# Moving six weight-chunk conversions out of the attention steps of a talking-heads + feed-forward kernel

## The chip, the cores and the metric

The kernel runs on one core of one Trainium2 chip. The metric is the device time of one execution in microseconds (us). The profile comes from one more execution, recorded by the hardware profiler.

## The reference

Two layers run one after the other. The first is "talking heads" attention over 4 batches, 12 heads, 448 positions and head size 64. The second is a feed-forward pair of products over the 1792 rows that attention gives:

```python
scores = scale * np.matmul(q, k.transpose(0, 1, 3, 2))
scores = np.einsum('bhij,hg->bgij', scores, w_pre)     # heads mixed
attn = softmax(scores)                                 # over the last axis
attn = np.einsum('bhij,hg->bgij', attn, w_post)        # mixed again
x = np.matmul(attn, v)                                 # -> 1792 x 768
h = x @ w_in                                           # 768 x 2048
g = where(h >= 1, h, where(h <= -1, 0, (h + 1)**2 / 4))
out = g @ w_out                                        # 2048 x 768
```

w_in and w_out arrive as doubles (8 bytes); everything else is float32.

## The kernel before

**Attention.** The 448 rows of a batch are cut into 4 tiles (120, 120, 120 and 88 rows), and each of the 16 tiles into 3 groups, which gives 48 *steps*. Step n does this, in this order on each engine: SyncE (SP) issues the transfers; TensorE (PE) mixes the heads of group n (`pre`, L221), takes the exponentials of group n-1 into the second mixing (`post`, L261), multiplies a finished tile by v (`pv`, L285), transposes q and k, and computes scores of a later tile (`scores`, L184); VectorE (DVE) takes the row maxima (L225) and evicts; ScalarE (ACT) does the exponentials (L233) and evicts; GpSimd (POOL) adds a small number to the row sums (L240) and scales w_post by their reciprocals (`norm`, L243). The score rows of group n+1 are gathered from one SBUF place (`ssb`) to another (`srows`) by four transfers, `load_s` (L210), issued at the beginning of step n. The places of `srows` are 10, two and a half groups.

**Conversion of the weights.** [...] Each weight matrix is 16 chunks of 128 x 768, and each chunk is turned into float32 and written back to DRAM (`wsd` for w_in, `wod` for w_out). Chunk number 2f is part f of w_in, 2f+1 part f of w_out. One chunk takes, over three steps:

- step n, `conv_load` (L321): three DMAs of 256 KB each, issued by SP just behind `load_s`;
- step n+1: `conv_scaled` (ACT, L329), `conv_bits` (two DVE instructions, L342 and L343), `conv_low` (ACT, L334), `conv_rest` (an addition on POOL, L337);
- step n+2, `conv_store` (L348): one DMA of 384 KB, issued by SP.

The list `CS` (L302) says which steps load a chunk: before, steps 2 to 40 without 3, 6, 15, 18, 27, 30 and 39, so 32 steps for 32 chunks in their order.

**Queues.** All transfers of this part stand in SP's one queue. SP executes it in order: a DMA whose place is not yet free holds all behind it, and issuing a DMA itself takes SP time. The order of the work is written out by hand (`tc.manual_schedule()`); every engine executes its instructions in the order of the program.

**Feed-forward.** The first product is a Strassen-like scheme of 56 *products* j = 0 to 55 (`step(j)`, L514): four quarters of seven with 512 columns each, then four quarters of seven with 384 columns. With k = j mod 7, products 0, 2, 4, 6 of a quarter add into one accumulator bank, 3 and 5 into another. Product j+2 can't write its bank before `evict_f(j)` has read it: ACT does this for k = 0, 2, 3 (L574) and DVE for k = 1, 4, 5 (L576). Within the emission of product j stand, in order: the split of the weights for product j+2 into a high part (ACT, L403) and a low part (DVE, L406), the gates (ACT L542 to L550, DVE L553 to L559), sums of weights and rows (DVE L439, L469), splits of x, and last the eviction. POOL does nothing here. The second product (`mults`, L679) follows, 1176 matmul groups over w_out; it reads parts 10 to 15 of w_out only after it has begun.

Of the kernel before, what the change touches and what calls it, by code (L numbers as in the profile page):

```python
# [11 lines left out]
I32 = mybir.dt.int32  # L12
U32 = mybir.dt.uint32
I64 = mybir.dt.int64
# [8 lines left out]
def tile_talking_heads_moe(  # L23
# [23 lines left out]
    NF = DFF // 128  # L47
    CW = 384
# [12 lines left out]
    qp = s_qk.enter_context(tc.tile_pool(name="qk", bufs=2, side="right"))  # L61
# [14 lines left out]
    for b in range(B):  # L76
        for i0 in range(0, S, QT):
            t = len(tiles)
            n = min(QT, S - i0)
# [6 lines left out]
            if n > 4 * IH * np_:  # L86
                i = (n - 4 * IH * np_) // 2
# [4 lines left out]
    NG = len(groups)  # L92
# [206 lines left out]
        kept[t % 2] = nc.sync.dma_start(out=xd[:, :, b * S + i0:b * S + i0 + n], in_=xo.pop(t)[:, :, :n])  # L299


    CS = [n for n in range(2, NG - 7) if n % 12 not in (3, 6)]  # L302
    craw = {}
    cwt = {}
    cwk = {}

    def conv_ends(i):
        f = i // 2
        if i % 2:
            return w_out[f * 128:(f + 1) * 128, :], wod[f]  # L310
        return w_in[:, f * 128:(f + 1) * 128].rearrange("(k p) f -> p k f", p=128), wsd[f].rearrange("c p d -> p c d")

    def conv_load(i):
        craw[i] = qp.tile([128, 2 * CW], I64, tag="wraw", name="wraw", bufs=2)
        src = conv_ends(i)[0]
        x = craw[i].rearrange("p (k f) -> p k f", f=256 if i % 2 else 128)
        if i % 2:
            src = src.rearrange("p (k f) -> p k f", f=256)
        w = x.shape[1] // 3
        for k in range(0, 3 * w, w):  # L320
            nc.sync.dma_start(out=x[:, k:k + w], in_=src[:, k:k + w])  # L321

    def halves(i):
        w = craw[i].bitcast(I32).rearrange("p (n t) -> p n t", t=2)
        return w[:, :, 0], w[:, :, 1]

    def conv_scaled(i):
        cwt[i] = qp.tile([128, 2 * CW], I32, tag="wt", name="wt", bufs=3)
        nc.scalar.activation(out=cwt[i].bitcast(F32), in_=halves(i)[1].bitcast(F32), func=AF.Copy,  # L329
                             scale=2.0 ** -111)  # L330

    def conv_low(i):
        cwk[i] = qp.tile([128, 2 * CW], I32, tag="wk", name="wk", bufs=1)
        nc.scalar.activation(out=cwk[i], in_=halves(i)[0].bitcast(U32), func=AF.Copy, scale=2.0 ** -29)  # L334

    def conv_rest(i):
        nc.gpsimd.tensor_tensor(out=cwt[i], in0=cwt[i], in1=cwk.pop(i), op=ALU.add)  # L337

    def conv_bits(i):
        hi = halves(i)[1]  # L340
        t = cwt[i]
        nc.vector.tensor_single_scalar(out=t, in_=t, scalar=3, op=ALU.logical_shift_left)  # L342
        nc.vector.scalar_tensor_tensor(out=t, in0=hi, scalar=-0x80000000, in1=t,  # L343
                                       op0=ALU.bitwise_and, op1=ALU.bitwise_or)

    def conv_store(i):
        x = cwt.pop(i).bitcast(F32)
        nc.sync.dma_start(out=conv_ends(i)[1], in_=x if i % 2 else x.rearrange("p (c d) -> p c d", c=2))  # L348

    def conv(n, f):  # L350
        if n in CS and CS.index(n) < 2 * NF:
            f(CS.index(n))


    NA = 1024
# [7 lines left out]
    raw = {}  # L363
# [7 lines left out]
    def view(name, p, off, *dims, dt=F32):  # L371
        n = 1
        for d in dims:
            n *= d
        named[name] = named.get(name, -1) + 1
        x = nc.alloc_sbuf_tensor_at(f"{name}_p{named[name]}", [128, n], dt, offset=area[p] + off).ap()
        if len(dims) == 2:
            x = x.rearrange("p (a b) -> p a b", b=dims[1])
        return x
# [51 lines left out]
    def split_w(j):  # L431
        if j < NJ:
            wts[j] = split_to(raw[KIND[j % 7], j // 7] if j < NJA else raw.pop(j))
# [86 lines left out]
    def step(j):  # L520
        q, k = divmod(j, 7)
        ph = j // NJA
        if k in (0, 1, 3):
            bk[BANK[k]] = bank(3 * (q % 2) if k == 0 else k // 2 + 1)[:, :, :NH[ph]]
        w = wts.pop(j)
        for s in range(2):
            product(bk[BANK[k]][:, s, :], w, s, [xop[ph, k, r] for r in range(3)], k in (0, 1, 3))

    def slot(q, i, h):
        ph = q // NQ  # L530
        return gq[ph, q % NQ].rearrange("p (n i) t -> p n i t", i=2)[:, :, i, h * NH[ph]:(h + 1) * NH[ph]]
# [24 lines left out]
    def take_maxima():  # L556
        while maxima:
            d, x, a = maxima.popleft()
            nc.vector.tensor_tensor(out=d, in0=x, in1=a, op=ALU.max)  # L559
# [5 lines left out]
    def evict_f(j):  # L565
        q, k = divmod(j, 7)
        o = bk[BANK[k]]
        if k == 6:
            bk[q] = o
            return  # L570
        d = slot(q, *((0, 0), (0, 0), (0, 1), (1, 1), (1, 1), (0, 1))[k])
        if k in (0, 2, 3):
            for s in range(2):
                nc.scalar.activation(out=d[:, s], in_=o[:, s, :], func=AF.Copy)  # L574
        else:
            nc.vector.tensor_tensor(out=d, in0=o, in1=d, op=ALU.add)  # L576


    UNITS = ((0, 256), (256, 256), (1024, 256), (1280, 128))
    VOFF = (512, 512, 384, 384)  # L580
# [144 lines left out]
    with tc.manual_schedule():  # L725
# [23 lines left out]
        for m in range(2):  # L749
            x = masks[:, m]  # L750
# [99 lines left out]
        def sx(name, r, k):  # L850
            return lambda: split_xa(name, r, k)
# [24 lines left out]
        for n in range(NG + 2):  # L876
            if n == NE:
# [5 lines left out]
                    name="ps_h", bufs=1, space=PSUM, side="right", reuse_waits="tile"))  # L883
# [15 lines left out]
            j = 0  # L899
# [64 lines left out]
        for j in range(NJ):  # L964
            q, k = divmod(j, 7)
            ph = j // NJA
            end = q == NQ - 1
            if j:
                step(j)
                split_w(j + 2)  # L970
                take_maxima()
            else:
                evict_f(0)
            if k == 0 and q:
                gate_slot(q - 1, 1, 0)
            elif k == 1 and q:
                if ph == 0:
                    sum_w("A21", "A22", "A11", ALU.subtract, q)
                gate_slot(q - 1, 0, 1)
            elif k == 3:  # L980
                gate_slot(q, 0, 0, q not in (0, NQ - 1, NQ))
            elif k == 4 and q:
                gate_slot(q - 1, 1, 1, True)
            if j == 0:
                sum_w("S1", "A21", "A22", ALU.add, 0)
                sx("B12", 2, 4)()
                sx("B11", 2, 3)()
                x_last(2)
                for r, s in enumerate(("s4", "s2", "s6")):
                    load_xa("B22", r, s)  # L990
            elif j == 1:
                sum_w("A21", "A22", "A11", ALU.subtract, q)
            elif j == 2:
                for r in range(3):
                    split_xa("B22", r, 5)
            elif j == 3:
                for r in range(3):
                    split_xa("B21", r, 6)
            if ph == 0:
                if k == 0:  # L1000
                    keep_w(2, q)
                    keep_w(3, q)
                elif k == 2:
                    sum_w("A12", "A12", "A11", ALU.subtract, q)
                    keep_w(4, q)
                    load_b(NJA) if end else load_a("A11", q + 1)
                elif k == 3:
                    keep_w(5, q)
                    load_b(NJA + 1) if end else load_a("A21", q + 1)
                elif k == 4:  # L1010
                    if end:
                        load_b(NJA + 2)
                        load_b(NJA + 3)
                    else:
                        load_a("A22", q + 1)
                        load_a("A12", q + 1)
                elif k == 5 and not end:
                    sum_w("S1", "A21", "A22", ALU.add, q + 1)
                elif k == 6 and not end:
                    sum_w("A11", "S1", "A11", ALU.subtract, q + 1)  # L1020
            load_b(j + 6) if j + 2 >= NJA else None
            if 4 <= j < 7:
                tx_load(j - 4)
            if 6 <= j < 18:
                tx_sum(j - 6)
            if 7 <= j < 19:
                tx_keep(j - 7)
            if 19 <= j < 22:
                for p in range(4):
                    load_xb(4 * (j - 19) + p)  # L1030
            for x in XAT.get(j, ()):
                split_xb(x)
            if j:
                evict_f(j)
            f = j - NJ + 3
            if f == 0:
                load_t(0)
                load_t(1)
            elif f == 1:
                split_t(0)  # L1040
                load_t(2)
                prep_s(0)
            elif f == 2:
                split_t(1)
                load_t(3)
                prep_s(1)
# [62 lines left out]
```

## Time and profile before

| what | us |
|---|---|
| three runs | 862.22, 852.49, 862.94 (median 862.22) |
| profiled execution, its device time | 856.64 |
| its span, first to last instruction | 854.9 |
| attention and the change to the next part, about | 0 to 463 |
| feed-forward, first product, from its last wait but one | 463.5 to 647.3 |
| feed-forward, second product | 647.3 to 854 |
| PE busy | 803.0 (94%) |
| DVE busy | 626.2 (73%) |
| ACT busy | 500.8 (59%) |
| POOL busy | 116.4 (14%) |

PE is the engine that is busy longest. Its busy time is pipelined time: a matmul that waits inside the pipeline counts as busy. The part of the span in which PE could be quicker lies in attention, where its busy share is lower than later.

### The profile page before, as it was taken

The numbers are of one execution on the slowest core, as the hardware profiler recorded it, in microseconds if no ns is written. First come the engines' busy times: TensorE is split into PE (matmuls) and PEld (weight loads), VectorE is DVE, ScalarE is ACT, GpSimd is POOL, SyncE is SP. The second block draws the span as 40 slices with busy tenths as digits, with TensorE's granted clock in tenths as the row PEclk, the third lists the DMA queues.
The fourth block names the chain that finished last, engine by engine and source line by source line (L and its number), as shares of the span: only waits on it lengthen the run. The fifth ranks groups of instructions, "written<-read, shape, count | busy, mean of one in ns | idle before, by whom it ended". The sixth has DMA issues, their size and how long they took to land.

```text
span 854.9 us, 26184 instructions
## 1 busy us (share of the span) xinstructions
PE 803.0 (94%) x11274; PEld 667.4 (78%) x11274; DVE 626.2 (73%) x751; ACT 500.8 (59%) x895; POOL 116.4 (14%) x147
## 2 busy tenths in 40 slices
PE   8799998989989989889789999999999999999998
PEld 6467765667656667557677888899999999999998
DVE  4777876667776767766498797996659978677763
ACT  4576765667666667757545646786666444433431
POOL 4022232222332213322130000000000000000000
PEclk9999999999999999999899999999999999999999
DMA  7688788889889997885826647644433633123331
GB/s 151 201 252 225 235 239 271 255 237 247 249 263 277 238 240 242 269 276 189 242 82 219 243 145 239 207 136 127 127 126 130 222 129 125 54 91 111 124 117 65
DMA packets 139091, 162.87 MB, mean 191 GB/s; under 512 B 42252, under 2 KB 128480, under 8 KB 138976
## 3 DMA queue, kind: packets, MB, share of 16 engines
q1 hardware_dynamic: 138464, 160.50, 61.8%
q8 instruction: 89, 1.46, 0.7%
q0 software_dynamic: 256, 0.47, 0.3%
q10 hardware_dynamic: 256, 0.23, 0.1%
q14 instruction: 26, 0.21, 0.1%
HBM read 88.81 MB, written 33.82 MB: 143 GB/s over the span
## 4 chain that ended last, share of the span: by engine, by line
PE 71%; DMA 11%; ACT 5%; DVE 5%; SPq 4%; issue 3%; POOLq 1%; POOL 0%; ACTq 0%; DVEq 0%
PE ps_f L679 24%; PE ps_f L514 21%; DMA srows<-ssb 8%; PE ps_a L261 7%; PE ps_l L221 6%; PE ps_x L285 5%; PE ps_s L184 4%; ACT e L233 2%; SPq L210 2%; PE ps_k L148 2%; DVE nm L225 1%; DMA kraw<-in_k_dram 1%; SPq L321 1%; DVE ssb L190 1%; PE ps_t L169 1%
## 5 line engine op out<-in xcount | busy, mean ns | idle before, releaser
L233 ACT ACTIVATE e<-ps_l,nm 128x448 f32<-128x448 f32 x180 | 112.0, 632 | 52.4 <-DVE nm L225 52.0
L261 PEld LDWEIGHTS ps_a<-wr,e 60*64 60x64 f32 (+1 forms) x5760 | 103.5, 129 | 48.2 <-issue 26.9
L225 DVE TENSOR_REDUCE nm<-ps_l 128x2 f32<-128x896 f32 (+1 forms) x92 | 95.3, 1063 | 41.9 <-PE ps_l L221 38.1
L261 PE MATMUL ps_a<-wr,e 60*64 60x60 f32 (+2 forms) x5760 | 111.9, 219 | 14.8 <-ACT e L233 7.4
L221 PE MATMUL ps_l<-srows,wpre 64*64 64x448 f32 (+2 forms) x720 | 101.8, 561 | 16.4 <-DMA srows<-ssb 7.6
L662 ACT ACTIVATE sgh_p<-gq_p 128x1024 fp32r<-128x1024 f32 (+1 forms) x56 | 53.3, 953 | 89.8 <-PE ps_f L679 89.6
L406 DVE SCALAR_TENSOR_TENSOR wl<-wi,wh 128x768 fp32r<-128x768 f32 x71 | 67.7, 953 | 41.9 <-ACT wh L403 41.9
L679 PE MATMUL ps_f<-wh,sgl_p 128*128 128x384 f32 x294 | 98.2, 334 | 0.0
L679 PE MATMUL ps_f<-wh,sgh_p 128*128 128x384 f32 x294 | 98.2, 334 | 0.0
L679 PE MATMUL ps_f<-wl,sgh_p 128*128 128x384 f32 x294 | 98.2, 334 | 0.0
L403 ACT ACTIVATE wh<-wi 128x768 fp32r<-128x768 f32 x71 | 59.7, 842 | 57.8 <-DVE wi L626 18.0
L663 DVE TENSOR_TENSOR sgl_p<-gq_p,sgh_p 128x1024 fp32r<-128x1024 f32 (+1 forms) x56 | 60.9, 1088 | 35.0 <-ACT sgh_p L662 35.0
L221 PEld LDWEIGHTS ps_l<-srows,wpre 64*64 64x64 f32 (+2 forms) x720 | 26.6, 134 | 70.2 <-issue 18.5
L285 PE MATMUL ps_x<-aT,v 112*64 112x120 f32 (+1 forms) x1408 | 77.3, 262 | 2.4 <-issue 2.4
L192 ACT ACTIVATE aT<-ps_a 112x960 f32<-112x960 f32 (+1 forms) x44 | 41.8, 950 | 53.0 <-PE ps_a L261 52.7
L285 PEld LDWEIGHTS ps_x<-aT,v 112*64 112x64 f32 x1408 | 67.9, 137 | 5.7 <-issue 3.1
L190 DVE COPY ssb<-ps_s 120x896 f32<-120x896 f32 (+1 forms) x48 | 52.0, 1084 | 22.8 <-PE ps_s L184 14.0
L337 POOL TENSOR_TENSOR wt<-wt,wk 128x768 int32<-128x768 int32 x32 | 58.1, 1816 | 53.3 <-ACT wk L334 51.4
L190 DVE COPY aT<-ps_a 112x960 f32<-112x960 f32 x48 | 55.0, 1145 | 3.0 <-PE ps_a L261 3.0
L679 PEld LDWEIGHTS ps_f<-wh,sgh_p 128*128 128x128 f32 x294 | 55.2, 188 | 0.0
L679 PEld LDWEIGHTS ps_f<-wl,sgh_p 128*128 128x128 f32 x294 | 55.2, 188 | 0.0
L679 PEld LDWEIGHTS ps_f<-wh,sgl_p 128*128 128x128 f32 x294 | 55.2, 188 | 0.0
(211 smaller groups left out, 1653.1 us busy)
## 6 DMA issues: line engine op xcount, KB each, us to landing
srows<-ssb SPq DMA_DIRECT2D x176, 210.0 KB
wraw<-in_moe_w_in_dram SPq DMA_DIRECT2D x48, 256.0 KB
wraw<-in_moe_w_out_dram SPq DMA_DIRECT2D x48, 256.0 KB
wi<-wod SPq DMA_DIRECT2D x29, 384.0 KB
wi<-wsd SPq DMA_DIRECT2D x28, 384.0 KB
wsd<-wt SPq DMA_DIRECT2D x16, 384.0 KB
wod<-wt SPq DMA_DIRECT2D x16, 384.0 KB
wi<-wss SPq DMA_DIRECT2D x16, 384.0 KB
```

The source lines that it names most:

```text
L190: nc.vector.tensor_copy(out=out, in_=in_)
L221: nc.tensor.matmul(out=ps[h, j, :S], lhsT=wpre[p], rhs=x[p], start=True, stop=True)
L225: nc.vector.tensor_reduce(out=nm, in_=lps[m][:, :k, :S], axis=AX.X, op=ALU.max, negate=True)
L233: nc.scalar.activation(out=e, in_=ps[:, j, :S], func=AF.Exp, bias=nm[:, j:j + 1], accum_out=sm[:, j:j + 1])
L261: nc.tensor.matmul(out=o[h, r, :, :n, j], lhsT=e[p, r * KP + h.start:r * KP + h.stop], rhs=w[p].rearrange("p (g i) -> p g i", i=IH)[:, :, :n],
L285: nc.tensor.matmul(out=ps[half[s], m, :n], lhsT=vt[b, g][:, 2 * m + s, r * D:(r + 1) * D], rhs=a[:KP, r * H + h, :n], start=(r == 0), stop ...
L337: nc.gpsimd.tensor_tensor(out=cwt[i], in0=cwt[i], in1=cwk.pop(i), op=ALU.add)
L403: nc.scalar.activation(out=hi, in_=t, func=AF.Copy, scale=2.0 ** -8)
L406: nc.vector.scalar_tensor_tensor(out=lo, in0=t, scalar=2.0 ** -8, in1=hi.bitcast(F32), op0=ALU.mult, op1=ALU.subtract)
L514: nc.tensor.matmul(out=o, lhsT=u[:, c, k], rhs=x, start=first and r == 0 and m == 0, stop=r == 2 and m == 2, skip_group_check=True)
L663: nc.vector.tensor_tensor(out=lo, in0=src, in1=hi.bitcast(F32), op=ALU.subtract)
L679: nc.tensor.matmul(out=o, lhsT=x[:, f, c], rhs=y[:, f % 2, :], start=first and f == 0 and m == 0, stop=hf == 1 and f == 3 and m == 2, skip ...
```

## The change

Ten of w_out's chunks stay in attention, placed between w_in's 16 by a list `CONV`; the last six, parts 10 to 15, are converted during the first feed-forward product by `late_conv(j)`, called in the emission of product j behind `evict_f(j)`. Steps divisible by three no longer load a chunk: against before, steps 9, 12, 21, 24, 33 and 36 lose theirs, and the 26 others stay. The late chunks use fixed SBUF places that no other tile holds at that time; the intermediate of `conv_low` is written in place, over the low halves of the doubles.

```diff
-    CS = [n for n in range(2, NG - 7) if n % 12 not in (3, 6)]
+    LATE = 6
+    CONV = [2 * f for f in range(NF)]
+    for f in range(NF - LATE):
+        CONV.insert(2 * f + 2 + f // 2, 2 * f + 1)
+    CS = [n for n in range(2, NG - 7) if n % 3]
...
-        if n in CS and CS.index(n) < 2 * NF:
-            f(CS.index(n))
+        if n in CS:
+            f(CONV[CS.index(n)])
...
+    RAWS = (("gg", 32768), ("gg", 49152), ("gg", 58368), ("xc", 12288), ("xc", 18432))
+    LOWS = (("gg", 38912), ("gg", 55296), ("gg", 55296), ("xc", 9216), ("xc", 9216))
+    LCONV = ((7, 10, 0), (9, 13, 1), (12, 17, 2), (27, 30, 3), (30, 34, 4), (34, 38, 3))
+
+    def late_conv(j):
+        for m, (j0, j1, x) in enumerate(LCONV):
+            i = 2 * (NF - LATE + m) + 1
+            if j == j0:
+                conv_load(i, view("cr", *RAWS[x], 2 * CW, dt=I64))
+            elif j == j1:
+                conv_scaled(i, view("ct", *LOWS[x], 2 * CW, dt=I32))
+                conv_bits(i)
+            elif j == j1 + 1:
+                conv_low(i, halves(i)[0])
+                conv_rest(i)
+            elif j == j1 + 2:
+                conv_store(i)
...
             if j:
                 evict_f(j)
+            late_conv(j)
```

## Rows read from the trace of the kernel before

**Rows 1.** The page: shares of the span of the chain that ended last.

```profile
PE 71%; DMA 11%; ACT 5%; DVE 5%; SPq 4%; issue 3%; POOLq 1%; POOL 0%; ACTq 0%; DVEq 0%
```

**Rows 2.** Windows between the L240 of steps 3, 12, 16, 24, 28; 36, 40, 42.

```profile
core 0: us, PE busy (x) PEld busy (x) DVE busy (x) ACT busy (x) POOL busy (x), PEclk, DMA share, GB/s
49.69:122.58 72.89, 70.35 (x1753) 52.00 (x1753) 56.28 (x72) 53.45 (x109) 20.85 (x25) 1.00 0.82 239
122.58:161.94 39.36, 33.03 (x699) 21.90 (x697) 27.05 (x34) 24.47 (x54) 11.11 (x13) 0.96 0.81 254
161.94:232.70 70.76, 66.77 (x1571) 47.77 (x1570) 50.81 (x64) 47.91 (x98) 18.05 (x23) 1.00 0.90 249
232.70:270.18 37.48, 32.28 (x700) 21.01 (x698) 26.85 (x34) 24.16 (x54) 11.16 (x13) 1.00 0.84 264
...
342.43:379.96 37.53, 32.20 (x699) 21.54 (x699) 26.87 (x35) 24.34 (x54) 11.03 (x13) 0.95 0.85 268
379.96:394.79 14.83, 14.53 (x382) 10.61 (x382) 11.13 (x14) 10.85 (x24) 3.60 (x5) 1.00 0.63 207
```

**Rows 3.** Timeline of SP: start us, us, what it issues and how many.

```profile
115.12 4.40 SPq L321 DMA_DIRECT2D wraw<-in_moe_w_out_dram  x3
...
120.10 0.45 SPq L348 DMA_DIRECT2D wod<-wt  x1
120.65 4.54 SPq L210 DMA_DIRECT2D srows<-ssb  x4
125.29 2.75 SPq L321 DMA_DIRECT2D wraw<-in_moe_w_in_dram  x3
```

**Rows 4.** The chain that ended last, pieces in order: start us, us, what.

```profile
21.22 4.90 DMA srows<-ssb
...
124.42 5.30 DMA srows<-ssb
```

**Rows 5.** Tiles wraw and wt, SP's issues: count, ns minimum/median/maximum, first and last start.

```profile
L321 SPq DMA_DIRECT2D wraw<-in_moe_w_out_dram x48: 356/846/2063, 50.8 to 377.4; - x48
...
L348 SPq DMA_DIRECT2D wod<-wt x16: 326/448/1607, 73.0 to 394.0; - x16
```

**Rows 6.** The page, DMA issues: count, KB each.

```profile
wraw<-in_moe_w_out_dram SPq DMA_DIRECT2D x48, 256.0 KB
...
wod<-wt SPq DMA_DIRECT2D x16, 384.0 KB
```

**Rows 7.** Tile wt: the conversion's instructions, columns as in Rows 5.

```profile
L329 ACT ACTIVATE wt<-wraw x32: 884/906/942, 49.5 to 387.2; 128x768 f32<-128x768 f32 x32
L342 DVE TENSOR_SCALAR wt<-wt x32: 525/528/560, 50.7 to 389.2; 128x768 int32<-128x768 int32 x32
L343 DVE SCALAR_TENSOR_TENSOR wt<-wraw,wt x32: 1022/1224/1360, 51.3 to 389.8; 128x768 int32<-128x768 int32 x32
L337 POOL TENSOR_TENSOR wt<-wt,wk x32: 1799/1817/1837, 53.6 to 392.2; 128x768 int32<-128x768 int32 x32
```

**Rows 8.** Windows as in Rows 2: products 14 to 20, and products 28 to 34.

```profile
500.85:529.67 28.82, 28.82 (x127) 23.62 (x126) 23.20 (x27) 17.29 (x21) 0.00 (x0) 1.00 0.56 194
...
558.49:580.33 21.84, 21.84 (x128) 21.84 (x127) 20.40 (x28) 16.59 (x25) 0.00 (x0) 1.00 0.41 125
```

**Rows 9.** Timeline of DVE about products 39 to 41: start us, us, what, idle before.

```profile
595.70 0.96 DVE L406 SCALAR_TENSOR_TENSOR wl<-wi,wh 128x768 fp32r<-128x768 f32 x1 [3.21 <-ACT wh L403]
...
597.45 0.95 DVE L576 TENSOR_TENSOR gq_p<-ps_f,gq_p 128x768 f32<-128x768 f32 x1
```

**Rows 10.** Timeline of PE: the first matmul of product 41.

```profile
599.05 0.34 PE L514 MATMUL ps_f<-b6h_p,wl 128*128 128x384 f32 x1
```

**Rows 11.** Timeline of POOL: two of the instructions that scale w_post.

```profile
117.08 0.55 POOL L243 TENSOR_TENSOR wr<-wpost,rs 128x120 f32<-128x120 f32 x1 [1.42 <-DVE rs L241]
...
125.51 0.74 POOL L243 TENSOR_TENSOR wr<-wpost,rs 128x240 f32<-128x240 f32 x1 [2.70 <-DVE rs L241]
```

**Rows 12.** Timeline of DVE at the same two places.

```profile
117.42 1.02 DVE L343 SCALAR_TENSOR_TENSOR wt<-wraw,wt 128x768 int32<-128x768 int32 x1
...
125.84 1.22 DVE L343 SCALAR_TENSOR_TENSOR wt<-wraw,wt 128x768 int32<-128x768 int32 x1
```

More of the change, by code (lines that the diff above doesn't have):

```diff
@@ L311, in conv_ends, with conv_load @@
         return w_in[:, f * 128:(f + 1) * 128].rearrange("(k p) f -> p k f", p=128), wsd[f].rearrange("c p d -> p c d")
-    def conv_load(i):
-        craw[i] = qp.tile([128, 2 * CW], I64, tag="wraw", name="wraw", bufs=2)
+    def conv_load(i, raw=None):
+        craw[i] = qp.tile([128, 2 * CW], I64, tag="wraw", name="wraw", bufs=2) if raw is None else raw
         src = conv_ends(i)[0]
@@ L325, in halves, with conv_scaled, conv_low @@
         return w[:, :, 0], w[:, :, 1]
-    def conv_scaled(i):
-        cwt[i] = qp.tile([128, 2 * CW], I32, tag="wt", name="wt", bufs=3)
+    def conv_scaled(i, t=None):
+        cwt[i] = qp.tile([128, 2 * CW], I32, tag="wt", name="wt", bufs=3) if t is None else t
         nc.scalar.activation(out=cwt[i].bitcast(F32), in_=halves(i)[1].bitcast(F32), func=AF.Copy,
                              scale=2.0 ** -111)
-    def conv_low(i):
-        cwk[i] = qp.tile([128, 2 * CW], I32, tag="wk", name="wk", bufs=1)
+    def conv_low(i, k=None):
+        cwk[i] = qp.tile([128, 2 * CW], I32, tag="wk", name="wk", bufs=1) if k is None else k
         nc.scalar.activation(out=cwk[i], in_=halves(i)[0].bitcast(U32), func=AF.Copy, scale=2.0 ** -29)
```

## The prediction

> **What bounds the kernel now.** Start with the page's chain of waits: PE has 71% of it, but DMA 11% and SP's queue 4% [rows 1]. So some of the end is set by transfers and by their issue, and the question is where. The windows cut at step boundaries answer it [rows 2]. Steps 40 and 41, where the DMA share is down to 0.63, take 14.83 us, 7.4 us each, and PE fills them. Four such steps would be 29.7 us. But the four steps from 12 take 39.36, those from 24 take 37.48 and those from 36 take 37.53 [rows 2]: 9.7, 7.8 and 7.8 us over PE's own pace, 25.3 us in three places I call the *zones*. Outside them there is less to win: 72.89 us from step 3 to 12 with PE busy 70.35, and 70.76 with 66.77 from 16 to 24 (the stretch from 28 to 36 is like it).
>
> Why the zones are slow shows in SP's timeline [rows 3]: a store, four gathers and three chunk loads follow one another without a pause, 0.45, 4.54 and 2.75 us, and the chunk before took 4.40. A step's transfers alone fill 8 us or more of SP's queue, against PE's 7.4. The gather of srows stands on the chain [rows 4], and it is issued late because chunk transfers stand ahead of it. The DMA engines are busy too: share 0.81 to 0.85, at 254 to 268 GB/s [rows 2]. Either way PE waits for srows, and a chunk is what makes the step too full.
>
> In the first feed-forward product it is the reverse: PE busy 28.82 of 28.82 and 21.84 of 21.84, DMA share 0.56 and 0.41, POOL idle, but DVE busy 23.62 and 20.40 [rows 8]. Here every microsecond of PE stall goes to the end.
>
> **What is removed, part by part.** Steps 12, 24 and 36 lose a chunk inside a zone; 9, 21 and 33 three steps ahead of one. A chunk costs SP three loads and a store: at the medians 3 x 0.846 + 0.448 = 2.99 us [rows 5], at the fullest place 4.40 + 0.45 = 4.85 [rows 3]. For the DMA engines it is 3 x 256 + 384 KB, 1.18 MB [rows 6], which at 264 GB/s [rows 2] take 4.5 us. The ACT, DVE and POOL work of those steps goes as well, but none of them is full there (24.47, 27.05 and 11.11 of 39.36 [rows 2]), so I give it nothing; it lies beside the wait for srows, and if that wait went entirely, PE would be next.
>
> Bounds: at least the zone's own chunk at the lower price, 3 x 2.99 = 9 us; at most all six at 4.5, 27 us, which is also about all that the zones have (25.3). I take for each zone its own chunk at 4.5, because SP and DMA are both full there, and half of 2.99 for the chunk three steps earlier, because SP still has some waits in those steps and its lead is limited by the ten places of srows: 6 us a zone, **18 us** in all, nearer the middle.
>
> The reordering (w_in's chunks sooner, w_out's late) costs nothing: w_in is complete at step 42, as before, and w_out's last parts are read only in the second product, after 647 us; were that cover gone, PE would wait there for a chunk's transfers, about the 4.5 us above.
>
> **What is added.** Six conversions beside the first product. Each brings two ACT passes (0.906 us each), 0.528 + 1.224 us on DVE, 1.817 us on POOL [rows 7], and four DMAs. The transfers I cost at nothing: shares of 0.56 and 0.41 leave room [rows 8], and the loads are issued three or more products ahead of their use. The store makes SP wait for POOL, and behind it stand weight loads for products at least two ahead; POOL needs 1.8 us of a product's 28.82 / 7 = 4.1, so it should be done when SP arrives. If not, one product waits, 3 to 4 us.
>
> ACT and DVE are another matter, since they execute in program order. Take products 38 to 41 [rows 9, 10]. DVE idles 3.21 us until ACT has split the weights for product 41, at 595.70; it then evicts product 39 at 597.45 to 598.40, and product 41 needs that bank at 599.05. The slack is 0.65. The change puts `conv_scaled` ahead of ACT's split (0.9 us later) and `conv_bits` ahead of DVE's low part: 1.75 us, which begin only when ACT has scaled, near 595.7. The eviction then ends some 1.8 us later, and PE stalls for 1.8 - 0.65 = 1.15 us. The places at products 10 and 17 have the same k = 3 and the same order; I give them the same. Three places make 3.5 us; for the three others (13, 30, 34), where no such tight eviction follows at once, 0.5 together. **4 us.**
>
> Then POOL. L343 reads two SBUF tensors. Beside a POOL instruction that ended at 126.25 it ended at 127.06; beside one that ended at 117.63, at 118.44 [rows 11, 12]. Both times it ends 0.81 us after POOL does, and takes 1.22 or 1.02 accordingly: it was held until POOL had finished. In attention the longer addition L337 falls beside DVE instructions that read PSUM. In the first product most of DVE's work reads two SBUF tensors, so L337's 1.82 us can hold it. Two or three of the six additions will fall into a DVE pause like the 3.21 us of [rows 9]; the others, where DVE is busy 23.20 of 28.82 or 20.40 of 21.84 [rows 8], delay it by up to 1.82 each. Three of them: 5.5, of which I take **5 us**.
>
> The Trainium skill's page "SBUF — State Buffer", section "SBUF: two separate sides", speaks against this change: VectorE and GpSimd share one pair of ports as an exclusive lock, and a VectorE instruction with two SBUF inputs and a GpSimd instruction that reads SBUF shut each other out for their whole length. The trace agrees [rows 11, 12]. If every one of the six additions shut DVE out and all of that reached PE, the cost would be 6 x 1.82 = 10.9 instead of 5 and the sum 854; without the lock it would be 843.
>
> Bounds of what is added: 0, if all is hidden (PE can't gain here, it is full), and 6 x (2 x 0.906 + 1.752 + 1.817) = 32 us, if nothing is.
>
> **Sum.** 856.64 - 18 + 4 + 5 = 847.6, say 848 us. That is against the profiled execution, which lies 5.6 us below the median of the three runs and 4.2 above the lowest.
>
> **The rivals.**
>
> *Everything comes off and POOL holds nobody.* Attention gains 26, the product loses only 4: 856.64 - 26 + 4 = 835. For it: the zones have room for 25 us. Against: the chunk of step 9 lies where PE is already busy 70.35 of 72.89 [rows 2], and rows 11 and 12.
>
> *The gather's own latency remains.* A gather took 4.90 us at the very start, when little else was in flight, and 5.30 in the zone [rows 4]; what is left to win by less traffic is 0.4. If issue is not what delays it, each zone gains only half a chunk's issue, 1.5, and the whole 4.5: 856.64 - 4.5 + 9 = 861. Against it: the pauseless SP queue [rows 3].
>
> *Slower: DVE's queue in the first product.* Evictions, low parts and gates all stand behind the late conversions and behind POOL's lock. If the delays don't drain before the next chunk, each costs its whole 5.4 us: 32 us, and 856.64 - 18 + 32 = 871; with attention's gain at its lower bound 880. It decides from 3 us of stall a chunk on (18 / 6). For it: DVE at 20.40 of 21.84 in products 28 to 34, which hold two of the six. Against: DVE has pauses in the other quarters.
>
> *The change doesn't do what it says:* the late chunks' places are not free, SP is held at product 7, and weight loads behind it come late. Attention's work on PE ends before product 1, so this is unlikely; a stall of three products would give 860.
>
> **How the numbers follow.** Forecast 0.52 (its own range 841 to 857, from 9 to 24 us gained and 3 to 12 lost), all comes off 0.20, latency remains 0.17, slower 0.08, held places 0.03. The 2% are about what a measurement of this kernel can tell from no change: 17 us, so below 839.5 or above 873.8 on the profiled execution's basis. Faster by more: the second case and the edge of the first, 0.25. Slower by more: the upper half of the slower case, 0.05. Between: 0.70. The range for 8 in 10 runs from 836 to 864: it takes in the forecast, the latency case and half of the case of 835, and leaves out the other half and the slower case.
>
> **What would show it.** In the changed kernel's windows the zones should shrink from 39.4, 37.5 and 37.5 us to about 33, with pauses in SP's timeline before the steps divisible by three; the stretch from step 3 to 12 should stay near 73. Between products 11 and 42 PE should show stalls of 0.5 to 2 us, released by DVE's evictions or low parts, 9 us together, and L406 or L439 instructions stretched beyond 0.95 us beside L337. I am wrong if the zones stay at 37 or more, if the first product's stalls pass 18 us, or if they are nearly absent.

## The result, and the profile of the changed kernel

| | kernel before | changed kernel |
|---|---|---|
| median of 20 runs, us | 861.88 (852.05 to 866.61) | 852.35 (845.89 to 859.67) |
| ratio, 95% interval | | 0.9909 (0.9883 to 0.9936) |
| profiled execution, us | 856.64 | 857.77 |
| its span, us | 854.9 | 856.1 |

The change takes off 0.9%, 9.5 us between the medians, and the interval leaves out 1. **The two profiled executions don't show it**: before's lies 5.2 us below its median, the changed kernel's 5.4 above. Stages have to be compared, and over several profiles.

The windows are cut as in [rows 2]; behind the six of attention, from step 3 to step 40, stands one from the first matmul of product 7 to that of product 55. Columns as there.

```profile
48.19:129.34 81.15, 73.18 (x1758) 54.76 (x1760) 54.83 (x71) 52.15 (x108) 18.80 (x24) 0.96 0.76 213
129.34:163.57 34.23, 31.55 (x694) 20.56 (x694) 25.20 (x32) 22.55 (x52) 9.13 (x11) 1.00 0.85 255
163.57:235.34 71.77, 66.83 (x1578) 49.51 (x1578) 49.21 (x63) 46.02 (x96) 16.05 (x21) 0.98 0.81 229
235.34:271.32 35.98, 30.66 (x699) 21.19 (x699) 25.01 (x33) 22.45 (x52) 9.15 (x12) 0.95 0.82 247
271.32:335.61 64.29, 62.87 (x1573) 46.84 (x1574) 48.92 (x63) 46.09 (x96) 16.07 (x22) 1.00 0.86 247
335.61:369.69 34.08, 29.86 (x694) 20.90 (x693) 25.18 (x32) 22.61 (x52) 9.15 (x11) 1.00 0.86 250
464.12:645.14 181.02, 173.97 (x866) 156.30 (x864) 148.81 (x168) 124.93 (x176) 11.86 (x6) 0.99 0.60 197
```

The zones went from 39.36, 37.48 and 37.53 [rows 2] to 34.23, 35.98 and 34.08. The first stretch is 8 us longer, at a granted clock of 0.96. The last row is the price: before, products 7 to 55 took

```profile
472.01:643.99 171.98, 171.02 (x865) 155.09 (x864) 134.55 (x156) 116.06 (x164) 0.00 (x0) 1.00 0.51 166
```

so 9.04 us were added there. PE waits (engine, line, what it waited for: us in all, times, longest) from product 7 to 55; before, one of 1.0 us for ACT's L574 stood there:

```profile
PE ps_f L518 <- DVE gq_p L580: 4.4, 4, 2.4
PE ps_f L518 <- ACT gq_p L578: 2.6, 2, 1.6
```

All releasers are evictions, DVE's and ACT's. The page's chain of waits, against [rows 1], says the same by shares: it can be followed back only over 46% of the span, the two products, and DVE, ACT, DMA and issue hold 11% of the span in it. Before, PE alone held as long a part (L514 21%, L679 24%).

```profile
PE 35%; DVE 5%; DMA 2%; issue 2%; ACT 2%; SPq 0%; DVEq 0%; ACTq 0%
```

**The order, at product 41.** DVE's timeline about products 39 to 41, to be laid beside [rows 9], and then PE's:

```profile
595.88 0.56 DVE L346 TENSOR_SCALAR ct_p<-ct_p 128x768 int32<-128x768 int32 x1 [3.14 <-ACT ct_p L333]
596.48 0.96 DVE L347 SCALAR_TENSOR_TENSOR ct_p<-cr_p,ct_p 128x768 int32<-128x768 int32 x1
597.35 0.95 DVE L410 SCALAR_TENSOR_TENSOR wl<-wi,wh 128x768 fp32r<-128x768 f32 x1
...
599.09 0.95 DVE L580 TENSOR_TENSOR gq_p<-ps_f,gq_p 128x768 f32<-128x768 f32 x1
```

```profile
600.10 0.45 PE L518 MATMUL ps_f<-b6h_p,wl 128*128 128x384 f32 x1 [0.74 <-DVE gq_p L580]
```

The conversion's two instructions come out of the pause first; the low part and the eviction follow 1.5 us later than they would, and product 41 waits 0.74 us for the eviction.

**The lock, at three additions.** POOL's timeline, and DVE's at the same places:

```profile
488.89 1.86 POOL L341 TENSOR_TENSOR ct_p<-ct_p,cr_p 128x768 int32<-128x768 int32 x1 [58.22 <-ACT cr_p L338]
...
521.46 1.88 POOL L341 TENSOR_TENSOR ct_p<-ct_p,cr_p 128x768 int32<-128x768 int32 x1 [18.87 <-ACT cr_p L338]
570.07 2.46 POOL L341 TENSOR_TENSOR ct_p<-ct_p,cr_p 128x768 int32<-128x768 int32 x1 [46.73 <-DMA cr_p<-in_moe_w_out_dram]
```

```profile
489.57 2.00 DVE L410 SCALAR_TENSOR_TENSOR wl<-wi,wh 128x768 fp32r<-128x768 f32 x1 [0.43 <-ACT wh L407]
...
522.09 2.06 DVE L410 SCALAR_TENSOR_TENSOR wl<-wi,wh 128x768 fp32r<-128x768 f32 x1 [0.88 <-ACT wh L407]
...
569.83 0.96 DVE L558 TENSOR_TENSOR gq_p<-gq_p,ga_p 128x768 f32<-128x768 f32 x1
570.70 3.18 DVE L466 TENSOR_TENSOR b6l_p<-xr_p,b6h_p 128x384 fp32r<-128x384 f32 x3
```

L410 takes 0.95 us elsewhere; beside POOL's addition it takes 2.00 and 2.06, and ends 0.8 us after POOL. At 570 the holding goes both ways: POOL's addition is itself 0.6 us longer, while L558 finishes, and the three L466 behind it take 3.18 us together instead of 1.49. That is the costliest place: product 34, which needs the bank that DVE evicts next (L580 at 574.68), waits until 575.68, and then runs at a lower clock. Windows of the changed kernel: products 28 to 34, to be laid beside [rows 8], and the wait and what follows it:

```profile
554.41:580.47 26.06, 23.68 (x127) 23.35 (x126) 24.90 (x32) 19.14 (x29) 2.46 (x1) 0.93 0.63 211
...
571.00:575.60 4.60, 2.29 (x14) 1.97 (x12) 4.60 (x6) 4.42 (x5) 1.53 (x1) 1.00 0.15 52
575.60:580.50 4.90, 4.82 (x19) 4.83 (x20) 3.95 (x6) 0.90 (x1) 0.00 (x0) 0.65 0.75 244
```

DVE is busy without a gap for 4.60 of 4.60 us, PE for 2.29; then the granted clock is 0.65 for 4.9 us. The quarter takes 26.06 us instead of 21.84. The lower clock is this profile's alone. In E2 and E12 (below), product 34 waits as long, but the 4.9 us behind the wait ran at 1.00, and the quarter took 24.5 us. E12's window:

```profile
573.80:578.70 4.90, 4.90 (x28) 4.90 (x29) 3.94 (x5) 1.21 (x2) 0.00 (x0) 1.00 0.82 245
```

### The profile page after: what moved, and what is told of

It is laid out like the page before. It is cut to its first block, busy times and chain, and to the rows that moved or that the text cites. A ratio compares the mean times of both kernels' runs of the same rounds, so it can differ in the third digit from the quotient of the medians.

```text
span 856.1 us, 26225 instructions
## 1 busy us (share of the span) xinstructions
PE 800.6 (94%) x11274; PEld 671.0 (78%) x11274; DVE 630.5 (74%) x751; ACT 499.9 (58%) x895; POOL 116.3 (14%) x147
## 5 line engine op out<-in xcount | busy, mean ns | idle before, releaser
L225 DVE TENSOR_REDUCE nm<-ps_l 128x2 f32<-128x896 f32 (+1 forms) x92 | 94.8, 1063 | 37.2 <-PE ps_l L221 35.8
L221 PE MATMUL ps_l<-srows,wpre 64*64 64x448 f32 (+2 forms) x720 | 91.6, 552 | 6.0 <-DMA srows<-ssb 2.5
L410 DVE SCALAR_TENSOR_TENSOR wl<-wi,wh 128x768 fp32r<-128x768 f32 x71 | 71.8, 1014 | 26.3 <-ACT wh L407 26.3
L285 PE MATMUL ps_x<-aT,v 112*64 112x120 f32 (+1 forms) x1408 | 79.8, 265 | 9.3 <-issue 9.3
L285 PEld LDWEIGHTS ps_x<-aT,v 112*64 112x64 f32 x1408 | 69.4, 139 | 12.6 <-issue 9.9
L243 POOL TENSOR_TENSOR wr<-wpost,rs 128x240 f32<-128x240 f32 (+2 forms) x48 | 37.1, 772 | 128.3 <-DVE rs L241 113.2
```

The lines of the kernel that those rows point to most:

```text
L221: nc.tensor.matmul(out=ps[h, j, :S], lhsT=wpre[p], rhs=x[p], start=True, stop=True)
L225: nc.vector.tensor_reduce(out=nm, in_=lps[m][:, :k, :S], axis=AX.X, op=ALU.max, negate=True)
L285: nc.tensor.matmul(out=ps[half[s], m, :n], lhsT=vt[b, g][:, 2 * m + s, r * D:(r + 1) * D], rhs=a[:KP, r * H + h, :n], start=(r == 0), stop ...
L410: nc.vector.scalar_tensor_tensor(out=lo, in0=t, scalar=2.0 ** -8, in1=hi.bitcast(F32), op0=ALU.mult, op1=ALU.subtract)
```

## The experiments

The time of each kernel is given as its ratio to the kernel before, run on the same chip. "Products" is the stretch from product 7 to 55 in its profile: 172.0 us before; with the change 181.0, and 179.4 in E12. The edits of E5, E6, E7 and E11 are shown against the kernel before, the others against the changed kernel; for E10 E1's edit comes with it. E1, E5, E6 and E10 leave chunks out, and their second product reads other parts of w_out in their place.

**E1. Attention's part alone.**

```diff
-            late_conv(j)
...
+        f -= 6 if f >= NF - LATE else 0      # wo() reads other parts
```

> The attention part of the change alone: 26 chunks in attention, none beside the first product; where the second product would read the last six parts of w_out it reads six other parts. Theory (attention gains 18 us, the late conversions cost 9): 862 - 18 = 844 us, the first product as before, 172 us from product 7 to 55. Rival (attention gains no more than the 9.5 us that the whole change measured, and the late conversions cost nothing in the median): 852 us. Second rival, lower bound of attention's gain, 9 us: 853.

0.9788 (0.9733 to 0.9842), 841.79 us: 18 us off. Products 172.0. Its zones took 32.6, 36.8 and 34.8. The window from step 28 to 36, of the kernel before and then of E1:

```profile
270.18:342.43 72.25, 66.49 (x1578) 48.20 (x1576) 50.76 (x65) 47.88 (x98) 18.02 (x22) 1.00 0.89 245
...
260.17:325.58 65.41, 63.50 (x1570) 47.13 (x1571) 48.78 (x62) 46.01 (x96) 16.04 (x21) 1.00 0.85 239
```

The size is the forecast's. The place isn't: this stretch, which was to have little to win, went from 72.25 to 65.41, and PE's busy time in it from 66.49 to 63.50.

**E2. The late conversions alone.** All 32 chunks in attention as before, and the six converted once more late.

```diff
...
-    CS = [n for n in range(2, NG - 7) if n % 3]
+    CONV = list(range(2 * NF))
+    CS = [n for n in range(2, NG - 7) if n % 12 not in (3, 6)]
```

> The late conversions alone: all 32 chunks in attention as before, and the six last parts of w_out converted a second time at the places of the change. Theory: the first product takes 9 us more from product 7 to 55 (172 to 181 us) and the kernel 862 + 9 = 871 us. Rival (late conversions hidden): 862 us. Rival (they cost their whole work, 5.4 us each): 894 us.

1.0096 (1.0060 to 1.0132), 8 us more; products 179.4. E1 and E2 multiply to 0.988, against 0.991 for the change: as far as these intervals tell, the two parts don't touch each other.

**E3. Without POOL's addition in the late chunks.**

```diff
-                conv_rest(i)
+                cwk.pop(i)
```

> The changed kernel with POOL's addition of the six late chunks left out (their lowest bits are missing); everything else stays, the two ACT passes and two DVE instructions too. Theory (POOL's additions hold DVE, 5 of the 9 us): the first product takes 176 us from product 7 to 55 instead of 181, the kernel 852 - 5 = 847 us; the stalls at products 18 to 19 and 33 to 34 shrink most, those at 13, 20 and 41 stay. Rival (only the order on ACT and DVE counts): 181 us and 852 us, no stall gone.

0.9902 (0.9857 to 0.9946), a time that can't be told from the change's. The products can: 175.7, and the waits in them (the same view as for the changed kernel) are

```profile
PE ps_f L518 <- DVE gq_p L580: 2.1, 4, 1.0
PE ps_f L518 <- ACT gq_p L578: 1.7, 3, 1.0
```

So the order costs 3.7 (175.7 - 172.0), and POOL's addition the rest, 3.7 to 5.3 by the three profiles with all of it (179.4, 179.4, 181.0). The 5.3 contains the lower clock behind product 34. By the spacing of the products, the addition reaches PE at two places only: product 19 begins 1.4 us sooner without it, and product 34 2.2 us.

**E4. The same six at other places**, three of them behind the eviction (the flag 1), three ahead of the split of the weights (0); the addition always behind the eviction.

```diff
+    LCONV = ((7, (10, 0), (12, 1), 0), (9, (14, 0), (16, 1), 1), (12, (19, 0), (19, 1), 2),
+             (27, (33, 1), (34, 1), 3), (30, (36, 1), (37, 1), 4), (35, (39, 1), (41, 1), 3))
```

> The changed kernel with the late conversions at other places: ACT and DVE passes ahead of the weights' split at products 10, 14 and 19 and behind the eviction at 33, 36 and 39; the low half with POOL's addition at 12, 16, 19, 34, 37 and 41, where DVE has pauses in the trace. The same work in all. Theory (the 9 us are a matter of where DVE is tight): stalls of 1 to 3 us instead of 9, 173 to 175 us from product 7 to 55, the kernel 852 - 7 = 845 us. Rival (the cost is the work itself on full engines): still 181 us and 852 us.

0.9863 (0.9799 to 0.9927); products 178.4, not clearly better. ACT's timeline after the chunk at product 14, ahead of product 19, which waits 1.7 us:

```profile
499.11 0.85 ACT L407 ACTIVATE wh<-wi 128x768 fp32r<-128x768 f32 x1 [3.73 <-DVE wi L443]
499.86 1.14 ACT L546 ACTIVATE ga_p<-gq_p,cs 128x1024 f32<-128x1024 f32 x1
...
503.19 1.07 ACT L578 ACTIVATE gq_p<-ps_f 128x512 f32<-128x512 f32 x2
```

In this stretch DVE has no pause, and POOL's addition, from 495.46 to 497.33, holds DVE as well:

```profile
495.81 2.34 DVE L410 SCALAR_TENSOR_TENSOR wl<-wi,wh 128x768 fp32r<-128x768 f32 x1
```

So DVE's weight sum L443 comes late, ACT's split waits 3.73 us for it, three gate passes follow, and only then the eviction (L578). A delay on DVE can come back by way of ACT's queue.

**E5 and E6. Which chunks count.** Before, without the chunks of steps 12, 24, 36 (E5) or 9, 21, 33 (E6).

```diff
+    CS = [n for n in range(2, NG - 7) if n % 12 not in (0, 3, 6)]   # E5
+    CS = [n for n in range(2, NG - 7) if n % 12 not in (3, 6, 9)]   # E6
```

> The kernel before with the chunks of steps 12, 24 and 36 left out alone (three parts of w_out are not converted; the second product reads other parts in their place). Theory of the prediction (a zone gains 4.5 us by its own chunk, 1.5 by the one three steps earlier): 13.5 of 18 us, 860 - 13.5 = 846 us. Rival (all six chunks are worth the same, 3 us each): 851 us. Rival (nothing but the sum of the traffic counts, and the gain is spread over the stretch behind): the zones shrink by less than 2 us each.

> The kernel before with the chunks of steps 9, 21 and 33 left out alone. Theory of the prediction: 4.5 of 18 us, 855 us. Rival (all six are worth the same): 851 us, as without 12, 24 and 36.

E5: 0.9963 (0.9927 to 0.9999), 3 us off. E6: 0.9892 (0.9848 to 0.9936), 9 us off. So the chunk three steps ahead is worth 3 us, twice what was forecast. The chunk inside a zone comes out at 1 instead of 4.5, but the two intervals overlap (0.9927 to 0.9936), and E8 below, with the same attention as E5, gives 3. That the second three are worth more than the first isn't shown.

**E7. SP relieved, bytes unchanged.** Before, with the chunk loads issued by POOL.

```diff
-            nc.sync.dma_start(out=x[:, k:k + w], in_=src[:, k:k + w])
+            nc.gpsimd.dma_start(out=x[:, k:k + w], in_=src[:, k:k + w])
```

> The kernel before with the three loads of every chunk issued by POOL instead of SP; the same bytes, the same steps, stores still on SP. If SP's issue time is what makes a step too full (2.54 us of it a chunk), the zones shrink by about 4 us each, PE's waits for srows go and the kernel is 10 us faster or more, 850 us. If the traffic on the DMA engines is what counts, the zones stay at 37 to 39 us and the kernel at 860 us. If POOL's queue adds waits of its own (behind the additions, or for w_post's scaling), it is slower than 860.

1.0222 (1.0189 to 1.0254), 19 us slower. SP's timeline in the first zone now has pauses, between 131.6 and 133.0 and after 133.4:

```profile
126.85 4.73 SPq L210 DMA_DIRECT2D srows<-ssb  x4
133.04 0.32 SPq L133 DMA_DIRECT2D qraw<-in_q_dram  x1
139.57 0.35 SPq L348 DMA_DIRECT2D wod<-wt  x1
```

and the zone takes 40.79 us all the same (39.36 before), with a granted clock of 0.87:

```profile
128.77:169.56 40.79, 34.75 (x706) 24.28 (x706) 26.98 (x34) 24.59 (x54) 16.62 (x22) 0.87 0.80 241
```

**E8 and E9. Fewer late chunks, in DVE's pauses.** E8 leaves steps 12, 24, 36 free and converts three chunks late. E9 leaves all six but step 24, and converts four chunks whole and one in two halves.

```diff
+    CS = [n for n in range(2, NG - 7) if n % 12 not in (0, 3, 6)]   # E8
+    LCONV = ((7, (10, 0), (12, 1), 0), (12, (17, 0), (19, 1), 2), (34, (38, 0), (40, 1), 3))
...
+    CS = [n for n in range(2, NG - 7) if n % 3 or n == 24]   # E9
+    LCONV = ((7, (10, 0), (12, 1), 0), (12, (17, 0), (19, 1), 2), (27, (33, 1), (34, 1), 3), (34, (38, 0), (40, 1), 4),
+             (43, (45, 0), (47, 1), "h0"), (49, (52, 0), (54, 1), "h1"))
```

> Three late chunks instead of six: steps 12, 24 and 36 lose theirs, and parts 13 to 15 of w_out are converted beside the first product ahead of the weights' split at products 10, 17 and 38 (the pauses of 3.2 to 3.6 us of DVE), POOL's additions at 12, 19 and 40. Theory: attention gains 13.5 us, the first product loses 1 to 2 us: 860 - 12 = 848 us, better than the change. Rival (all six worth the same): 860 - 9 + 1.5 = 852 us, no better than the change.

> Five late chunks, all in DVE pauses: whole chunks at products 10, 17, 33 and 38, one in two halves at 45 and 52 (ACT and DVE ahead of the weights' split except at 33, POOL's addition two products later, one at 33); step 24 keeps its chunk, the other steps divisible by three have none. Theory (attention gains 15 of 18 us; in the pauses a late chunk costs 0.4 us, as with three late ones, and 0.8 at 33): 860 - 15 + 3 = 848 us, 174 to 175 us from product 7 to 55, 4 us better than the change. Rival (late work costs what it costs wherever it stands, 1.5 us a chunk): 180 us in the first product, 852 us.

E8: 0.9908 (0.9874 to 0.9943), 8 us off, products 173.2. Up to product 7 its instructions are those of E5. E8 does 1.2 us more in the products and is still 4 to 5 us faster than E5, so its attention gained 9 us where E5's gained 3; why is open. With E8, the chunks inside the zones (9 us) and those ahead (E6, 9 us) add up to E1's 18, 3 us each. E9: **0.9842 (0.9795 to 0.9890), 846.83 us, the fastest of the kernels that do the whole work**; products 173.98 for five chunks. In time its interval overlaps that of the change, run beside it (E12); the products, 5.4 us fewer, are the clear part. DVE's timeline of E9 at products 10 to 12:

```profile
474.14 0.56 DVE L346 TENSOR_SCALAR ct_p<-ct_p 128x768 int32<-128x768 int32 x1
474.73 0.96 DVE L347 SCALAR_TENSOR_TENSOR ct_p<-cr_p,ct_p 128x768 int32<-128x768 int32 x1
...
479.76 0.96 DVE L410 SCALAR_TENSOR_TENSOR wl<-wi,wh 128x768 fp32r<-128x768 f32 x1 [2.73 <-ACT wh L407]
...
482.24 1.22 DVE L580 TENSOR_TENSOR gq_p<-ps_f,gq_p 128x1024 f32<-128x1024 f32 x1
...
484.68 2.95 DVE L563 TENSOR_TENSOR gq_p<-gq_p,ga_p 128x1024 f32<-128x1024 f32 x1
```

The bits now stand before the pause, and the pause is still 2.73 us long. The addition falls behind the eviction L580; it still holds DVE (L563 takes 2.95 instead of 1.21), but nobody waits for that.

**E10. The order of the chunks.** E1 with its chunks in the order of their numbers.

```diff
+    CONV = [i for i in range(2 * NF) if not (i % 2 and i > 2 * (NF - LATE))]
```

> As the run with the attention part alone, but the 26 chunks in the order of their numbers (w_in and w_out in turn), not w_in ahead. The removals of three steps each gave 3.2 and 9.3 us, 12.5 in sum, all six with the new order 18.2. Theory (order costs nothing, the gains of six don't add up from threes): 842 us. Rival (the order is worth the rest): 860 - 12.5 = 847 us.

0.9789 (0.9736 to 0.9841): the same as E1, within the 5 us of the interval either way. No cost and no gain of the reordering shows.

**E11. One load of 768 KB a chunk instead of three**, else before.

```diff
-        for k in range(0, 3 * w, w):
-            nc.sync.dma_start(out=x[:, k:k + w], in_=src[:, k:k + w])
+        nc.sync.dma_start(out=x, in_=src)
```

> The kernel before with one load of 768 KB a chunk instead of three of 256 KB; the same bytes. If SP's issue time makes the steps too full, SP is relieved by up to 1.7 us a chunk, the zones shrink by 2 us each and the kernel is 5 us or more faster, 855 us. If the DMA engines' traffic counts, the zones stay and the kernel stays at 860 us, or becomes slower where gathers come to stand behind one long transfer.

1.0106 (1.0057 to 1.0156), 9 us slower, zones 38.4, 44.0 and 39.6. Two issues fewer a chunk helped no more than E7's relief did.

**E12. The change again**, on the chip of E9 to E11.

> The changed kernel once more, on the same chip as the three others: 852 us, 181 us from product 7 to 55.

0.9908 (0.9870 to 0.9946), as at first; its stretch from step 3 to 12 took 76.2, not 81.2.

## Why the prediction was right, step by step

The forecast was 848 us, on the basis of a profiled execution 5.6 below the median then known. It said 9 us off (18 - 4 - 5); measured, 9.5 off the 861.88 of 20 runs. The 848 itself is 4 us low, by the profiled execution's place among the runs. The total is better than its parts. The terms:

- **Attention, 18 us.** E1: 18. The profiles agree once each is set to its own kernel's median. Product 7 began at 472.0 before and at 470.5 in E2, whose attention is the same. In the five kernels with the change's steps (the changed kernel, E1, E3, E4, E12) it began at 464.1, 455.4, 460.6, 452.2 and 462.4. From product 55 to the end all of these take 210.9 us, so what sets a profile off from its kernel's median lies ahead of that. With this distance added, the means are 476.6 and 460.4, 16 us apart.
- **Where in attention: wrong.** All of it was to come from the zones. Over those five profiles their mean is 34.4, 35.8 and 35.0, 105 in all, against 114.4 before and 111.7 in E2: 7 to 9 us. As much comes from the eight steps from 16 and the eight from 28: 69.4 and 65.4, 135 together, against 143.0 before and 141.5 in E2. Steps 21 and 33, which lose a chunk, lie in these two stretches. The step that failed was "Outside them there is less to win", read from PE busy 66.77 of 70.76. PE's busy time holds waits inside its pipeline: in E1 the eight steps from 28 took 65.41, less than before's *busy* time there (66.49). The pace of 7.4 us a step, from the same rows, would have said it: eight steps make 59, so each of these stretches had over 11 us to give.
- **Why in attention: the split per chunk was not borne out.** 4.5 us were given to a zone's own chunk and 1.5 to the one three steps ahead. E6 measured 3 for the second; for the first E5 gives 1 and E8 3. Nor did pauses appear in SP's timeline. The changed kernel's first zone:

```profile
124.30 4.29 SPq L210 DMA_DIRECT2D srows<-ssb  x4
...
129.43 4.55 SPq L210 DMA_DIRECT2D srows<-ssb  x4
134.08 3.16 SPq L325 DMA_DIRECT2D wraw<-in_moe_w_out_dram  x3
```

  SP is as pauseless as in [rows 3], and yet the zone is 5 us shorter; in E7 SP has pauses and the zone is no shorter. SP's issue time was not the limit that it looked like. (The transfers named there add up to 7.74 us, not to "8 us or more", hardly over PE's 7.4.) What E1, E7 and E11 leave is the bytes: less traffic helps, fewer issues for the same bytes don't. This isn't cleanly shown, because E7 and E11 also change where PE waits for instructions (last section), and E7 loads POOL. A rival stands beside it: with a chunk go its passes on ACT, DVE and POOL too, to which the forecast gave nothing. PE's waits for DVE's `ssb` fell from 6.2 to 1.5 us, those for the gathers from 7.4 to 2.2 (last section), and no run takes away the bytes without the passes.
- **The order of ACT and DVE, 4 us.** 3.7 (E3): 0.5 for the chunk at product 10, 1.8 at 17, 1.0 at 38 and 0.4 at 30, against 1.15 three times and 0.5 for the rest. The sum came out better than its parts. At product 41 the working held almost to the letter: 1.5 us late instead of 1.75, since L346 and L347 take 0.56 and 0.96, and a stall of 0.74 instead of 1.15. The 1.224 us of [rows 7] contained a wait behind POOL.
- **POOL's lock, 5 us.** 3.7 to 5.3 (E3). Three additions were to be felt at up to 1.82 each; PE felt two, 3.6 together. What brings the changed kernel's own profile to 5 is the lower clock, and that is luck. The places were not foreseen. The chunk at product 30, counted among three that cost 0.5 together, cost most: against the spacing of the products before, product 34 begins 2.55 us later and 35 another 1.68, the lower clock's part. With the chunks at 17 (3.1) and 38 (1.0) that is 8.4 of the 9.04. The first, at 10, cost 0.55 instead of 1.15.
- **Transfers and the store, 0.** None of PE's waits from product 7 to 55 was released by a DMA. The stretch from the L240 of step 47 to product 7 took 41.05 us, as before, so SP was not held at product 7.
- **The reordering, 0.** E10, within its interval.

By the Trainium skill's page "SBUF — State Buffer", section "SBUF: two separate sides", a GpSimd instruction that reads SBUF and a VectorE instruction with two SBUF inputs shut each other out for the whole instruction. The trace agrees: beside each of the six additions a DVE instruction is longer than elsewhere (L410 four times 2.00 to 2.07 us, the L466 at 570, and one L473 with 0.91 instead of 0.55). If all of this had reached PE, it would have been the 10.9 us of the prediction. E3 says that PE felt at most 5.3, and that at two places of six.

The rivals: 835 (all comes off, nobody held) fails at E3, and its attention part at E1; 861 (the gather's latency remains) at E1; the slower case at E2, which costs 1.4 us a chunk and not 3: away from products 13 and 14, 19 to 21, 34 and 35, 41 and 42 the products keep the spacing of before, so DVE's delays drain before the next chunk; the held places at the 41.05 us. Of the signs named, the pauses of SP were absent, the zones came to 34 to 36 us and not to 33, and "near 73" from step 3 to 12 held in part: it was 73.2, 76.1, 73.8 and 76.2 in E1, E3, E4 and E12 but 81.2 in the changed kernel's profile.

## What to carry to other kernels

Take the floor of a stretch from the fastest steps of the same kind, not from an engine's busy time, which can hold waits of its own; and test a "full queue" by emptying it before the gain is put down to it. Work moved into an in-order queue costs by its place: put it ahead of a pause that another engine causes, and behind the eviction that PE needs next (five chunks cost 2.0 us so, six at the change's places 7.4 to 9.0). When the effect is of the size of the spread between runs, compare stages over several profiles, each set to its own kernel's median. Before a few us are split up by cause, look whether two kernels that agree in that stage also agree in time: E5 and E8 don't, by 5 us.

## What the runs showed of the hardware

In attention PE has waits for which no semaphore accounts. PE's waits between 30 and 400 us, before and with the change (columns as above; "issue" is a wait that the profile puts down to nothing it shows):

```profile
PE ps_l L221 <- DMA srows<-ssb: 7.4, 15, 1.6
PE ps_l L221 <- DVE ssb L190: 6.2, 4, 3.1
PE ps_a L261 <- issue: 4.9, 5, 1.2
...
PE ps_x L285 <- issue: 2.4, 3, 1.3
```

```profile
PE ps_x L285 <- issue: 9.3, 7, 3.6
PE ps_a L261 <- issue: 8.6, 6, 3.8
...
PE ps_l L221 <- DMA srows<-ssb: 2.2, 6, 0.7
...
PE ps_l L221 <- DVE ssb L190: 1.5, 3, 0.7
```

The waits for srows and for ssb fell from 13.6 to 3.7 us, but those named issue rose from 7.3 to 17.9. One profile can't carry that: in E2, whose attention is that of before, they are 12.7, in E1 13.5, in E7 24.3. One of them made the changed kernel's long first stretch (PE's timeline):

```profile
72.36 1.63 PE L261 MATMUL ps_a<-wr,e 60*64 60x60 f32 x51 [3.80 <-issue]
73.92 3.47 PE L285 MATMUL ps_x<-aT,v 112*64 112x120 f32 x32
```

After 3.80 us of standing still, L285's 32 matmuls took 3.47 us, twice their usual 1.8. Windows of the standstill and of what follows show the clock:

```profile
68.50:72.30 3.80, 0.06 (x3) 0.00 (x0) 1.25 (x2) 2.90 (x9) 2.02 (x2) 0.85 0.69 163
72.30:77.50 5.20, 5.14 (x84) 4.71 (x84) 1.16 (x1) 0.00 (x0) 0.00 (x0) 0.50 0.28 104
```

The granted clock is 0.50 after the standstill, 1.2 of 2.4 GHz, and back at 1.00 in the window from 78 to 84 us; a pause of 3.8 us cost up to 2.6 us more in this window (half of 5.20, an estimate). Behind the 2.38 us at product 34 it was 0.65 for 4.9 us, but behind the 2.4 us at the same place in E2 and E12 it stayed at 1.00. The page lists beside the data a queue that brings instructions:

```profile
q8 instruction: 89, 1.46, 0.7%
```

That is 89 packets of 16 KB for PE's 11274 matmuls, one for some 127. In the second product, where they begin 22 us apart, 126 to 131 matmuls lie between two of them: the count fits PE's own instructions.

Laid beside the times of these packets in the traces, the waits have an answer. Between 30 and 460 us the 14 traces hold 142 waits of PE named issue of over 0.5 us, and every one ends 1.2 to 1.8 us after such a packet has ended. With 1001 packets in that time, one in 6 us, chance would put about a tenth of the waits there. In the standstill above, the packet ran from 69.45 to 70.70, after PE had stopped at 68.56, and PE went on at 72.36. So these are waits for instructions. Why a packet comes late isn't shown. That data on the same DMA engines hold it up would fit the growth in E7, the absence of such waits between products 7 and 55, and part of the spread between runs; no run isolates it.
